# First batch's attention in a fused attention and expert kernel: another order on TensorE, fewer empty products, and the first weight chunk's steps behind the sums

## The chip, the cores and the metric

The kernel runs on one core of one Trainium2 chip, in one launch. The metric is the device time of an execution in microseconds (us). TensorE is called PE in the rows, VectorE DVE, ScalarE ACT, GpSimd POOL, and SyncE, which issues most DMAs, SP.

## The reference, cut to what matters

Three stages follow each other: attention with two kinds of mask over 2 batches, 8 heads, 576 tokens and 64 columns a head; a bilinear layer; and four experts weighted by token.

```python
scores = scale * np.matmul(q, k.transpose(0, 1, 3, 2))
mask_local = (rel >= 0) & (rel < stride)                    # heads 0 to 3, stride 32
mask_strided = (rel >= 0) & (pos[None, :] % stride == pos[:, None] % stride)   # heads 4 to 7
attn = np.exp(scores - max) ; attn = attn / (attn.sum(-1) + 1e-09)
x = np.matmul(attn, v)                                      # 1152 tokens x 512
h = ((x @ w1) * (x @ w2)) @ w3 ;  x = h @ w_out             # 512 -> 1024 -> 1024 -> 512
out += p[:, e:e + 1] * (np.maximum(x @ w1[e], 0.0) @ w2[e]) # four experts
```

The weights of the bilinear layer (w1, w2, w3, w_out) come as 64-bit floats, while attention and experts have 32-bit inputs.

## The kernel before, in words

**Numbers.** Every large product is made of three: an operand is split into a high part (rounded for TensorE, `hi`) and the rest (`lo`), and `mm3` (lines 255 to 259) adds hi times hi, lo times hi and hi times lo into one PSUM bank.

**Weights.** 64-bit weights are worked on as pairs of 32-bit integers, 128 x 1024 at a time (class `Chunk`). The steps of a chunk are `raw_load` (a DMA of 1 MB into one of two `raw` buffers), `round_up` (ACT, L136, on the low words), `magnitude` (ACT, L144, on the high words; for the first chunk DVE, L142), then on DVE `clamp` (L147), `shift` (L150), `sign` (L153) and `add` (L157, which also issues the load of the chunk after next), then `split_hi` on ACT (L164, writes `w_hi`) and `split_lo` on DVE (L174, writes `w_lo`). The generator `work()` (L200) has all of these in one order, and `advance(n)` takes n steps of it wherever the program calls it. So the order on each engine is that of the program text: nothing is scheduled by cost. Chunks are numbered from 0 here; chunks 0 to 7 are w1 and w2 (`c_w12`).

**Attention.** A batch has six pieces (`Chunk4`): three local ones (numbers 0 to 2), then three strided ones (3 to 5). Steps of a piece: `scores` (PE, a mask product and 16 or 24 small ones), `maxima` (DVE, L356 and L361), `exps` (ACT, L367), `sums` (DVE, L374 or L376 to L378), `normalise` (L382; GpSimd in batch 0, DVE in batch 1), `transposes` (PE, L387), `evac` (ACT copies them out of PSUM, L392), `pv` (PE, weights by values, L404 or L413), `put` (ACT, L440, high part of x) and `put_lo` (DVE, L444, low part). `attend(b, s)` (L756) runs the pipeline's step s = 0 to 8: scores of piece s + 1, maxima and exps of s, sums and normalise of s - 1, pv and put of s - 3, transposes and evac of s - 2.

**Order of the work.** Nine steps of batch 0 come first, and in each, TensorE has the scores ahead of pv and transposes, and then some empty products (`keep_warm`, 102 of them in the nine steps after the 14 at the start). Between them `advance` does the first steps of the weights. Then come 32 units (`run_unit`, `ab_block`): unit 2c and 2c + 1 take batch 0 through chunk c, each with 24 products of 128 x 288; each unit takes two steps of the weights, and the steps of batch 1's attention stand after units 2, 4, 5, 7, 8, 10, 11, 13 and 14 (counted from 1). Units 16 to 31 take batch 1 through the chunks. The rest (w3 by w_out, the layer itself, the experts) is not touched.

```python
for k in range(4):
    mm3(acc, c_w12[ft].parts((w * 4 + k) * P, P), (x_hi[:, k, t], x_lo[:, k, t]), k == 0, k == 3)
```

**Limits that tie the engines.** There are 5 PSUM banks for pv, transposes, empty products and units, 3 for scores; each engine does its own instructions in order.

Of the kernel before, what the change touches and what calls it, by code (L numbers as in the profile page):

```python
# [18 lines left out]
P = 128  # L19
# [18 lines left out]
def flat(ap):  # L38
    return ap.rearrange("p a b -> p (a b)")
# [3 lines left out]
def kernel(  # L43
# [13 lines left out]
    nc = tc.nc  # L57
    mm = nc.tensor.matmul
# [13 lines left out]
    def bank(name):  # L72
        return ps.tile([P, 512], F32, tag="ps", name=name)
# [33 lines left out]
    def warm_up():  # L107

        idle = tmp.tile([P, P], F32, tag="pT", name="idle")
        nc.vector.memset(idle, 0.0)  # L110
        nc.scalar.activation(small.tile([P, 1], F32, tag="rec", name="one"), idle[:, :1], AF.Exp)
        zeros = idle.bitcast(BF16)

        def keep_warm(n):
            if n:
                acc = bank("idle")
            for i in range(n):
                mm(acc[:, :2 * P], zeros[:, :P], zeros, start=i == 0, stop=i == n - 1)

        keep_warm(WARM)  # L120
        return keep_warm


    class Chunk:
# [5 lines left out]
        def raw_load(self):  # L130
            self.raw = rawp.tile([P, 1024, 2], I32, tag="raw", name="raw64")
            nc.sync.dma_start(out=flat(self.raw), in_=self.src.bitcast(I32))

        def round_up(self):
            self.low, self.high = self.raw[:, :, 0], self.raw[:, :, 1]
            nc.scalar.activation(self.low, self.low.bitcast(U32), AF.Copy, scale=2.0 ** -29)  # L136

        def magnitude(self):
# [45 lines left out]
    c_w12 = [Chunk(w12[c]) for c in range(8)]  # L184
    c_wout = [Chunk(w_out[c]) for c in range(4)]
    c_w3 = [Chunk(w3T[c]) for c in range(8)]
    live = 8
# [13 lines left out]
    def work():  # L201


        wide = stream[:20]
        wide[0].round_up()
        wide[0].magnitude()
        yield True
        before = None
        for c, after in zip(wide, wide[1:] + [None]):
            if before:  # L210
                while live > 14:
                    yield False
                before.split_hi()
            c.clamp()
            yield True
            if before:
                before.split_lo()
            c.shift()
            yield True
            c.sign()  # L220
            yield True
            if after and c is not wide[0]:
                after.round_up()
                after.magnitude()
            c.add()
            yield True
            before = c
            if c is wide[0]:
                c.split_hi()
                after.round_up()  # L230
                yield True
                c.split_lo()
                yield True
                before = None
                after.magnitude()
        while live > 14:
            yield False
        before.split_hi()
        yield True
        before.split_lo()  # L240
        yield True
        for w in c_e:
            yield from w.work()

    worker = work()

    def advance(n=1):

        return all([next(worker, False) for _ in range(n)])
# [5 lines left out]
    def mm3(acc, lhs, rhs, first, last):  # L255
        (lh, ll), (rh, rl) = lhs, rhs
        mm(acc, lh, rh, start=first, stop=False)  # L257
        mm(acc, lh, rl, start=False, stop=False)  # L258
        mm(acc, ll, rh, start=False, stop=last)  # L259


    x_hi = xp.tile([P, 4, NT], F32R, tag="x_hi", name="x_hi")
    x_lo = xp.tile([P, 4, NT], F32R, tag="x_lo", name="x_lo")
# [185 lines left out]
    def ab_place(b, pair):  # L449
        ab_hi[b, pair] = big[b].tile([P, 2, S], F32R, tag="big", name="ab_hi")  # L450
        ab_lo[b, pair] = big[b].tile([P, 2, S], F32R, tag="big", name="ab_lo")
# [8 lines left out]
    def ab_block(b, ft, n):  # L460
        t = slice(b * S + n * HB, b * S + n * HB + HB)
        pair, late = ft // 2, b == 0 and ft < 6
        ab = tmp.tile([P, HB], F32, tag="pT", name="ab")
        if n == 0 and ft % 2 == 0:
            if late:
                whole[pair] = big[min(pair, 1)].tile([P, 2, S], F32, tag="big", name="ab_f32")
            else:
                ab_place(b, pair)
        if late:
            full = whole[pair][:, ft % 2, n * HB:n * HB + HB]  # L470
        else:
            full = ab
            hi, lo = (x[b, pair][:, ft % 2, n * HB:n * HB + HB] for x in (ab_hi, ab_lo))
        for w in range(2):
            acc = bank("ab_acc")[:, :HB]
            for k in range(4):
                mm3(acc, c_w12[ft].parts((w * 4 + k) * P, P), (x_hi[:, k, t], x_lo[:, k, t]), k == 0, k == 3)
            if w == 0:
                nc.scalar.copy(ab, acc)
            else:  # L480
                nc.vector.tensor_tensor(out=full, in0=acc, in1=ab, op=ALU.mult)
            yield
        if late:
            return
        nc.scalar.copy(hi, ab)
        yield
        nc.vector.tensor_tensor(out=lo, in0=ab, in1=hi.bitcast(F32), op=ALU.subtract)
        yield
# [126 lines left out]
    class Step:  # L615
# [22 lines left out]
        def add(self, out, acc, b):  # L638
            nc.vector.tensor_tensor(out=out, in0=acc, in1=b, op=ALU.add)  # L639

        def first(self, work):

            n = self.half.n
# [6 lines left out]
            self.product(b, "s2", "t2")  # L650
            self.add(u2, b, u1)
            work(1)
            self.product(c, "s3", "t3")
            self.add(u3, c, u2)
# [69 lines left out]
    with tc.manual_schedule():  # L724
        keep_warm = warm_up()
# [20 lines left out]
        chunks = [[Chunk4(3 * g + c, b, g, c) for g in range(2) for c in range(3)] for b in range(B)]  # L746
# [5 lines left out]
        def run_unit():  # L752

            nonlocal done, rest
            b, ft, i = units[done]
            need(c_w12[ft])  # L756
            block = ab_block(b, ft, i)
            for _ in range(2):
                next(rest, None)
                next(block)  # L760
                advance(1)
            rest = block
            done += 1
            if b == i == 1:
                c_w12[ft].free()

        def attend(b, s):

            nonlocal live
            chunk = chunks[b]  # L770
            n = len(chunk)
            if s == 0:
                chunk[0].scores()
            if s + 1 < n:
                chunk[s + 1].scores()
            if s < n:
                chunk[s].maxima()
                chunk[s].exps()
            if 1 <= s <= n:
                chunk[s - 1].sums()  # L780
                chunk[s - 1].normalise()
            if 3 <= s:
                c = chunk[s - 3]
                c.pv()
                c.put()
                c.put_lo()
                if c.g == 0 or b == 0 and c.c > 0:
                    live -= 1
            if 2 <= s < n + 2:
                chunk[s - 2].transposes()  # L790
                chunk[s - 2].evac(nc.scalar.copy)

        for s in range(9):
            attend(0, s)
            advance({4: 2, 5: 3, 6: 1, 7: 1}.get(s, 0))
            keep_warm({4: 20, 5: 14, 6: 12, 8: 16}.get(s, 8))
        advance(4)
        steps = iter(range(9))
        while done < 16:
            run_unit()  # L800
# [13 lines left out]
        for it in range(8):  # L814
# [8 lines left out]
            i = {1: 0, 3: 1, 6: 2}.get(it)  # L823
# [141 lines left out]
```

## Time and profile before

| what | value |
|---|---|
| time, median of 3 runs | 633.12 us (632.18 to 636.05) |
| the profiled execution's own time | 632.63 us |
| its span, first to last instruction | 630.7 us |
| TensorE clock granted, mean | 1.000 |
| busy: PE, DVE, ACT, POOL | 619.2, 450.7, 265.0, 9.9 us |
| moved by DMA | 99.45 MB, mean 158 GB/s |

The span lies inside the time of the execution, with 1.9 us around it. Busy time is a union over the engine's instructions; what an engine waited for is taken from the rows of single instructions.

### The profile page before, as it was taken

How to read it: one execution, taken by the hardware profiler on the slowest of the kernel's cores; microseconds unless marked ns; L12 is line 12 of the kernel's file. 1: busy time of each engine (PE TensorE's matmuls, PEld its weight loads, DVE VectorE, ACT ScalarE, POOL GpSimd, SP SyncE). 2: the span in 40 equal slices, each digit the busy share in tenths (PEclk: the TensorE clock that was granted, in tenths of full speed). 3: DMA queues.
4: the chain of work that ended last, by engine and by line, in shares of the span. 5: the costliest groups of instructions: out<-in, count | busy, mean ns of one | idle time of the engine just before them, and what ended most of it. 6: DMA issues, size and time to landing. Idle time of an engine off the chain costs nothing.

```text
span 630.7 us, 11461 instructions
## 1 busy us (share of the span) xinstructions
PE 619.2 (98%) x4706; PEld 566.1 (90%) x4706; DVE 450.7 (71%) x813; ACT 265.0 (42%) x455; POOL 9.9 (2%) x31
## 2 busy tenths in 40 slices
PE   8899999999999999999999999999999999999997
PEld 6699899999878999999988999898889999999996
DVE  4889996989775224867977887787875666765743
ACT  2555564765654223433344333344433333333320
POOL 4100000000000000000000000000000000000000
PEclk9999999999999999999999999999999999999999
DMA  9973432235442310345344353353497465556411
GB/s 295 268 240 129 135 130 73 77 135 179 147 134 73 128 68 0 134 146 189 133 156 179 134 201 134 136 197 134 143 330 278 150 253 187 212 194 209 137 63 68
DMA packets 28727, 99.45 MB, mean 158 GB/s; under 512 B 2652, under 2 KB 6740, under 8 KB 26116
## 3 DMA queue, kind: packets, MB, share of 16 engines
q1 hardware_dynamic: 28132, 98.14, 44.5%
q8 instruction: 37, 0.61, 0.4%
q10 hardware_dynamic: 544, 0.59, 0.3%
q14 instruction: 14, 0.11, 0.0%
HBM read 79.58 MB, written 19.14 MB: 157 GB/s over the span
## 4 chain that ended last, share of the span: by engine, by line
PE 86%; DVE 4%; ACT 4%; DMA 3%; issue 1%; SPq 1%; DVEq 0%
PE g_acc L257 10%; PE g_acc L258 10%; PE g_acc L259 10%; PE ab_acc L257 5%; PE ab_acc L259 5%; PE ab_acc L258 5%; PE m_a L257 4%; PE m_a L259 4%; PE m_a L258 4%; PE x_acc L257 3%; PE x_acc L258 3%; PE x_acc L259 3%; PE m_b L258 3%; PE m_c L257 3%; PE m_b L257 3%; PE m_c L258 3%
## 5 line engine op out<-in xcount | busy, mean ns | idle before, releaser
L633 ACT ACTIVATE h_hi<-u 128x320 fp32r<-128x320 f32 (+1 forms) x128 | 56.9, 445 | 188.5 <-DVE u L639 188.5
L257 PE MATMUL g_acc<-w_hi,h_hi 128*128 128x512 f32 (+1 forms) x296 | 114.3, 386 | 0.0
L258 PE MATMUL g_acc<-w_lo,h_hi 128*128 128x512 f32 (+1 forms) x296 | 114.2, 386 | 0.0
L259 PE MATMUL g_acc<-w_hi,h_lo 128*128 128x512 f32 (+1 forms) x296 | 113.7, 384 | 0.0
L639 DVE TENSOR_TENSOR u<-m_b,u 128x320 f32<-128x320 f32 (+1 forms) x96 | 40.8, 452 | 52.9 <-PE m_b L259 52.9
L572 DVE TENSOR_TENSOR w_lo<-raw,w_hi 128x768 fp32r<-128x768 f32 x64 | 69.3, 1083 | 12.0 <-ACT w_hi L570 11.9
L257 PE MATMUL ab_acc<-x_hi,w_hi 128*128 128x288 f32 x256 | 76.5, 299 | 1.1 <-ACT pT L392 1.0
L259 PE MATMUL ab_acc<-x_hi,w_lo 128*128 128x288 f32 x256 | 75.4, 294 | 0.0
L258 PE MATMUL ab_acc<-x_lo,w_hi 128*128 128x288 f32 x256 | 75.4, 294 | 0.0
L259 PEld LDWEIGHTS g_acc<-w_hi,h_lo 128*128 128x128 f32 x296 | 55.6, 188 | 11.6
L257 PEld LDWEIGHTS g_acc<-w_hi,h_hi 128*128 128x128 f32 x296 | 55.8, 188 | 8.0
L258 PEld LDWEIGHTS g_acc<-w_lo,h_hi 128*128 128x128 f32 x296 | 55.8, 188 | 7.6
L635 DVE SCALAR_TENSOR_TENSOR h_lo<-u,h_hi 128x320 fp32r<-128x320 f32 (+1 forms) x128 | 57.6, 450 | 3.5 <-ACT h_hi L633 1.7
L570 ACT CAST w_hi<-raw 128x768 fp32r<-128x768 f32 x64 | 59.9, 936 | 0.0
L257 PEld LDWEIGHTS ab_acc<-x_hi,w_hi 128*128 128x128 f32 x256 | 48.0, 188 | 1.8 <-ACT pT L392 1.2
L258 PEld LDWEIGHTS ab_acc<-x_lo,w_hi 128*128 128x128 f32 x256 | 48.1, 188 | 0.0
L259 PEld LDWEIGHTS ab_acc<-x_hi,w_lo 128*128 128x128 f32 x256 | 48.0, 188 | 0.0
L258 PE MATMUL m_b<-b_t,s_hi 128*128 128x320 f32 (+1 forms) x128 | 37.9, 296 | 0.0
L639 DVE TENSOR_TENSOR u<-m_a,u 128x320 f32<-128x320 f32 (+1 forms) x64 | 28.8, 451 | 11.6 <-PE m_a L259 11.6
L572 DVE TENSOR_TENSOR s_lo<-raw,s_hi 128x1024 fp32r<-128x1024 f32 x16 | 19.6, 1225 | 23.2 <-ACT s_hi L570 23.2
L136 ACT ACTIVATE raw<-raw 128x1024 int32<-128x1024 uint32 x20 | 23.4, 1171 | 29.2 <-DMA raw<-in_w3T_dram 19.0
L639 DVE TENSOR_TENSOR u<-m_c,u 128x320 f32<-128x320 f32 (+1 forms) x64 | 28.9, 452 | 4.7 <-PE m_c L259 4.0
(154 smaller groups left out, 1392.7 us busy)
## 6 DMA issues: line engine op xcount, KB each, us to landing
raw<-in_e_dram SPq DMA_DIRECT2D x32, 1024.0 KB
raw<-in_w_dram SPq DMA_DIRECT2D x8, 1024.0 KB
raw<-in_w3T_dram SPq DMA_DIRECT2D x8, 1024.0 KB
stored<-s_hi SPq DMA_DIRECT2D x16, 512.0 KB
stored<-s_lo SPq DMA_DIRECT2D x16, 512.0 KB
s_hi<-stored SPq DMA_DIRECT2D x16, 512.0 KB
s_lo<-stored SPq DMA_DIRECT2D x16, 512.0 KB
raw<-in_w_out_dram SPq DMA_DIRECT2D x4, 1024.0 KB
```

What stands on the lines that cost most here:

```text
L136: nc.scalar.activation(self.low, self.low.bitcast(U32), AF.Copy, scale=2.0 ** -29)
L257: mm(acc, lh, rh, start=first, stop=False)
L258: mm(acc, lh, rl, start=False, stop=False)
L259: mm(acc, ll, rh, start=False, stop=last)
L570: nc.scalar.copy(dst[0], src)
L572: nc.vector.tensor_tensor(out=dst[1], in0=src, in1=dst[0].bitcast(F32), op=ALU.subtract)
L633: nc.scalar.activation(hi, src, AF.Relu)
L635: nc.vector.scalar_tensor_tensor(out=lo, in0=src, scalar=0.0, in1=hi.bitcast(F32), op0=ALU.max, op1=ALU.subtract)
L639: nc.vector.tensor_tensor(out=out, in0=acc, in1=b, op=ALU.add)
```

## The change: what it does

In batch 0 each of the nine steps now has, on TensorE, pv of s - 3, transposes of s - 2, then scores of s + 1, and then the empty products: 6, 8, 12, 12 and 8 in steps 0, 5, 6, 7 and 8 and none in the others (46 in place of 102). `put` and `put_lo` stand behind `sums`, `normalise` and the steps of the weights. The first chunk's steps start in step 5 of the attention in place of step 4 (`magnitude`, `clamp` and `shift` in step 5, `sign` in 6, `add` in 7, `split_hi` and `split_lo` behind step 8), its `round_up` is called in step 6, and 10 steps in place of 11 are done when the units begin. The second chunk's `round_up` moves behind the first one's `split_lo`. The very first of the units' accumulations has its twelve products by kind: four hi by hi, four with x_lo, four with w_lo.

```diff
         def round_up(self):
-            self.low, self.high = self.raw[:, :, 0], self.raw[:, :, 1]
             nc.scalar.activation(self.low, self.low.bitcast(U32), AF.Copy, scale=2.0 ** -29)
...
         wide = stream[:20]
-        wide[0].round_up()
         wide[0].magnitude()
...
             if c is wide[0]:
                 c.split_hi()
-                after.round_up()
                 yield True
                 c.split_lo()
                 yield True
                 before = None
+                after.round_up()
                 after.magnitude()
...
-            for k in range(4):
-                mm3(acc, c_w12[ft].parts((w * 4 + k) * P, P), (x_hi[:, k, t], x_lo[:, k, t]), k == 0, k == 3)
+            parts = [(c_w12[ft].parts((w * 4 + k) * P, P), (x_hi[:, k, t], x_lo[:, k, t])) for k in range(4)]
+            if b == ft == n == w == 0:
+                for i, j in ((0, 0), (0, 1), (1, 0)):
+                    for k, (lhs, rhs) in enumerate(parts):
+                        mm(acc, lhs[i], rhs[j], start=i == j == k == 0, stop=i == 1 and k == 3)
+            else:
+                for k, (lhs, rhs) in enumerate(parts):
+                    mm3(acc, lhs, rhs, k == 0, k == 3)
...
+        first = chunks[0]
+        first[0].scores()
+        first[1].scores()
         for s in range(9):
-            attend(0, s)
-            advance({4: 2, 5: 3, 6: 1, 7: 1}.get(s, 0))
-            keep_warm({4: 20, 5: 14, 6: 12, 8: 16}.get(s, 8))
-        advance(4)
+            if 3 <= s:
+                first[s - 3].pv()
+            if 2 <= s < 8:
+                first[s - 2].transposes()
+            if 2 <= s + 1 < 6:
+                first[s + 1].scores()
+            keep_warm({0: 6, 5: 8, 6: 12, 7: 12, 8: 8}.get(s, 0))
+            if s < 6:
+                first[s].maxima()
+                first[s].exps()
+            if 1 <= s < 7:
+                first[s - 1].sums()
+                first[s - 1].normalise()
+            advance({5: 3, 6: 1, 7: 1}.get(s, 0))
+            if 3 <= s:
+                first[s - 3].put()
+                first[s - 3].put_lo()
+                if s != 6:
+                    live -= 1
+            if 2 <= s < 8:
+                first[s - 2].evac(nc.scalar.copy)
+            if s == 6:
+                c_w12[0].round_up()
+        advance(5)
```

**Place 1: TensorE in steps 2 and 3 of batch 0.** Before, with the scores of pieces 3 and 4 (`sc<-tk,tq 54x54`), the transposes of pieces 0 and 1 (`tp`), values of piece 0 (`o`) and one of each eight empty products:

```order
L343 MATMUL sc<-m_str,i_str 128x432
L350 MATMUL sc<-tk,tq 54x54 x16
L387 MATMUL tp<-ident,p_pair 128x128 x3
L118 MATMUL idle<-idle 128x256
L343 MATMUL sc<-m_str,i_str 128x432
L350 MATMUL sc<-tk,tq 54x54 x16
L404 MATMUL o<-pT,tv_loc 64x32 x24
L387 MATMUL tp<-ident,p_pair 128x128 x3
L118 MATMUL idle<-idle 128x256
```

The same two steps in the changed kernel:

```order
L386 MATMUL tp<-ident,p_pair 128x128 x3
L342 MATMUL sc<-m_str,i_str 128x432
L349 MATMUL sc<-tk,tq 54x54 x16
L403 MATMUL o<-pT,tv_loc 64x32 x24
L386 MATMUL tp<-ident,p_pair 128x128 x3
L342 MATMUL sc<-m_str,i_str 128x432
L349 MATMUL sc<-tk,tq 54x54 x16
```

The scores moved behind the transposes and values of their step, and the empty products of both steps are gone.

**Place 2: ACT around the rounding and magnitude of chunk 6, between units.** Before (`raw_1104` is chunk 6's buffer, `p_pair` the exps of batch 1's piece 4, `x_hi` and `pT` the put of piece 1 and the copy of piece 2's transposes, `ab` a unit's copy, `w_hi` chunk 5's):

```order
L136 ACTIVATE raw_1104<-raw_1104 128x1024
L144 ACTIVATE t<-raw_1104 128x1024
L367 ACTIVATE p_pair<-p_pair 128x8x54
L440 CAST x_hi<-o 128x2x3x32 x2
L392 COPY pT<-tp 128x384
L479 COPY ab<-ab_acc 128x288
L164 CAST w_hi<-t 128x1024
```

In the changed kernel, where chunk 6's buffer is `raw_1059`:

```order
L366 ACTIVATE p_pair<-p_pair 128x8x54
L439 CAST x_hi<-o 128x2x3x32 x2
L391 COPY pT<-tp 128x384
L484 COPY ab<-ab_acc 128x288
L136 ACTIVATE raw_1059<-raw_1059 128x1024
L144 ACTIVATE t<-raw_1059 128x1024
L164 CAST w_hi<-t 128x1024
```

The rounding and the magnitude moved behind the attention's exps, put and copy and behind a unit's copy.

**Place 3: DVE around chunk 6's low part, ahead of unit 12.** Before (`t` of the first row is chunk 7's clamp, `w_lo` is chunk 6's, `rec` and `p_pair` are the sums and normalise of batch 1's piece 5, `x_lo` is piece 3's):

```order
L147 TENSOR_SCALAR t<-t 128x1024
L481 TENSOR_TENSOR ab_f_1305<-ab_acc,ab 128x288
L174 TENSOR_TENSOR w_lo<-t,w_hi 128x1024
L150 TENSOR_SCALAR t<-t 128x1024
L374 TENSOR_REDUCE rec<-p_pair 128x8
L378 RECIPROCAL rec<-rec 128x8
L382 TENSOR_TENSOR p_pair<-p_pair,rec 128x8x54
L444 TENSOR_TENSOR x_lo<-o,x_hi 128x6x18 x4
```

In the changed kernel, with chunk 6's `add` as the first row:

```order
L157 ISA t<-raw_1059,t 128x2048
L486 TENSOR_TENSOR ab_f_1239<-ab_acc,ab 128x288
L147 TENSOR_SCALAR t<-t 128x1024
L373 TENSOR_REDUCE rec<-p_pair 128x8
L377 RECIPROCAL rec<-rec 128x8
L381 TENSOR_TENSOR p_pair<-p_pair,rec 128x8x54
L443 TENSOR_TENSOR x_lo<-o,x_hi 128x6x18 x4
L174 TENSOR_TENSOR w_lo<-t,w_hi 128x1024
L150 TENSOR_SCALAR t<-t 128x1024
```

The low part moved behind seven instructions of the attention; chunk 3's stands in the same way behind the maxima of piece 2 and the sums and normalise of piece 1. From the end of batch 1's attention on, the order is the same as before on every engine.

## Rows read from the trace of the kernel before

**Rows 1.** Stretches: length; PE, PEld, DVE, ACT, POOL busy; clock; DMA share; GB/s.

```profile
0.00:34.00 34.00, 29.85 (x622) 23.79 (x623) 21.91 (x50) 15.28 (x35) 9.68 (x29) 1.00 0.93 284
...
47.00:97.40 50.40, 48.81 (x683) 46.24 (x683) 49.09 (x84) 29.93 (x53) 0.23 (x2) 1.00 0.38 127
100.00:140.00 40.00, 40.00 (x304) 40.00 (x303) 32.15 (x50) 24.59 (x39) 0.00 (x0) 1.00 0.28 97
```

**Rows 2.** Timeline, TensorE, batch 0: start, us, instruction, [idle before, releaser].

```profile
16.80 0.91 PE L350 MATMUL sc<-tk,tq 64*18 64x18 f32 x32
...
18.17 0.90 PE L404 MATMUL o<-pT,tv_loc 64*64 64x32 f32 x47 [0.43 <-issue]
...
25.02 1.25 PE L118 MATMUL idle<-idle 128*128 128x256 bf16 x10 [1.44 <-issue]
...
31.52 0.90 PE L413 MATMUL o<-pT,tv_str 54*64 54x54 f32 x32 [0.66 <-ACT pT L392]
...
32.35 1.92 PE L118 MATMUL idle<-idle 128*128 128x256 bf16 x16
...
34.03 0.38 PE L257 MATMUL ab_acc<-x_hi,w_hi 128*128 128x288 f32 x1
```

**Rows 3.** Timeline, other engines, batch 0.

```profile
9.98 0.83 POOL L382 TENSOR_TENSOR p_pair<-p_pair,rec 128x384 f32<-128x384 f32 x1 [4.71 <-DVE rec L378]
...
16.97 0.61 DVE L361 TENSOR_TENSOR p_pair<-sc,mx 128x432 f32<-128x432 f32 x1
...
21.94 0.61 DVE L361 TENSOR_TENSOR p_pair<-sc,mx 128x432 f32<-128x432 f32 x1
22.46 0.60 DVE L374 TENSOR_REDUCE rec<-p_pair 128x8 f32<-128x440 f32 x1
...
24.94 1.22 DVE L153 SCALAR_TENSOR_TENSOR t<-raw,t 128x1024 int32<-128x1024 int32 x1
...
28.10 1.10 DVE L444 TENSOR_TENSOR x_lo<-o,x_hi 128x108 fp32r<-128x108 f32 x4
28.17 1.05 ACT L164 CAST w_hi<-t 128x1024 fp32r<-128x1024 f32 x1
...
29.12 1.15 ACT L136 ACTIVATE raw<-raw 128x1024 int32<-128x1024 uint32 x1
...
30.83 0.63 ACT L392 COPY pT<-tp 128x512 f32<-128x512 f32 x1
...
32.46 0.67 ACT L440 CAST x_hi<-o 128x108 fp32r<-128x108 f32 x4 [0.99 <-PE o L413]
```

**Rows 4.** Timeline, DVE, beside the units.

```profile
44.36 0.56 DVE L361 TENSOR_TENSOR p_pair<-sc,mx 128x384 f32<-128x384 f32 x1
45.53 0.69 DVE L147 TENSOR_SCALAR t<-t 128x1024 f32<-128x1024 f32 x1 [0.61 <-ACT t L144]
...
47.18 1.23 DVE L174 TENSOR_TENSOR w_lo<-t,w_hi 128x1024 fp32r<-128x1024 f32 x1 [0.49 <-ACT w_hi L164]
...
83.53 1.21 DVE L174 TENSOR_TENSOR w_lo<-t,w_hi 128x1024 fp32r<-128x1024 f32 x1
...
86.66 1.20 DVE L444 TENSOR_TENSOR x_lo<-o,x_hi 128x108 fp32r<-128x108 f32 x4
```

**Rows 5.** Timeline, ACT, beside the units.

```profile
43.33 1.16 ACT L136 ACTIVATE raw<-raw 128x1024 int32<-128x1024 uint32 x1 [3.80 <-DMA raw<-in_w_dram]
44.38 1.12 ACT L144 ACTIVATE t<-raw 128x1024 f32<-128x1024 f32 x1
45.41 0.51 ACT L367 ACTIVATE p_pair<-p_pair 128x384 f32<-128x384 f32 x1
45.82 0.38 ACT L479 COPY ab<-ab_acc 128x288 f32<-128x288 f32 x1
```

**Rows 6.** Timeline, TensorE: values and transposes ahead of unit 11.

```profile
82.28 0.82 PE L413 MATMUL o<-pT,tv_str 54*64 54x54 f32 x32 [0.61 <-ACT pT L392]
83.04 0.66 PE L387 MATMUL tp<-ident,p_pair 128*128 128x128 f32 x4
```

More of the change, by code (lines that the diff above doesn't have):

```diff
@@ L132, in raw_load @@
             nc.sync.dma_start(out=flat(self.raw), in_=self.src.bitcast(I32))
+            self.low, self.high = self.raw[:, :, 0], self.raw[:, :, 1]
         def round_up(self):
-            self.low, self.high = self.raw[:, :, 0], self.raw[:, :, 1]
             nc.scalar.activation(self.low, self.low.bitcast(U32), AF.Copy, scale=2.0 ** -29)
```

## The prediction

> **What bounds the kernel now.** I read the stretches first, then the waits, then single rows in order of time. The page's 98% for TensorE hides three regimes. In the first 34 us (batch 0's attention) no engine is full: TensorE shows 29.85 us, of which 102 empty products are part, DVE 21.91 [rows 1]. It is a loop through all engines: scores, maxima, exps, sums, normalise on GpSimd, transposes, copy, values, put. From 47 to 97.4 us DVE is busy for 49.09 of 50.40 us while TensorE has only 1.6 us idle: both are nearly full, and the weights' steps and batch 1's attention share DVE [rows 1]. From 100 to 140 us TensorE is full and DVE has 7.85 us idle: TensorE sets the pace there [rows 1]. So the change works in the first regime, and what it gains must be carried through the second, where DVE has nothing to give away.
>
> **The head, part by part.** 56 empty products go, at 0.125 us each (1.25 us for ten [rows 2]) 7 us of TensorE; most of it lay beside the loop. Where they stood on the path: ten at 25.02 and sixteen at 32.35, ahead of the first unit at 34.03 [rows 2]. I walk the new order with the rows' durations. Nothing moves until GpSimd has normalised piece 0, at 10.8 [rows 3]. Transposes (0.55) go first now, then the scores of piece 3 (0.91 and about 0.4 for the mask [rows 2]): they end at 12.75, and DVE subtracts piece 3 by 14.05, which is some 0.8 later than before. This is the price of the new order. Sums 1.0, low parts of piece 0 0.6 and maxima 0.6 bring the subtraction of piece 4 to 16.25, before 16.97 [rows 3]; the next cycle (subtraction, 0.5 of exps [rows 5], put 0.54, low part, maxima) brings piece 5 to 19.15, before 21.94 [rows 3]. DVE then has sums (0.6 [rows 3] and 0.25 for the reciprocal), magnitude, clamp and shift (0.7 each, as the clamp of [rows 4]), low part of piece 2 (0.6), sums (0.8): 24.0; sign 1.22 [rows 3], low part of piece 3 1.1 [rows 3], add 1.22: 27.4. That is when it ended before too (24.94 and twice 1.22 [rows 3]), so the load of chunk 2 that it issues, and the loads of batch 1's values behind that on SP, start when they did. Beside it: normalise 24.15 to 25.0, transposes 0.66 [rows 6], copy 0.63 [rows 3] behind piece 4's put to 26.6; the twelve empty products ahead of the last values wait for a PSUM bank (low part of piece 3) and end at 27.2; values 0.9 to 28.1, put 0.67 to 28.75, and now `w_hi` stands behind that put on ACT: 1.05 to 29.8 [rows 3]. First product at 29.85 in place of 34.03: 4.2 us early. `w_lo` comes at 31.07, behind the first eight products by kind, which end at 30.9; without the new order of these twelve TensorE would stand from the third one on, some 0.9 us. So unit 0 ends at 33.25, 4.0 early.
>
> An unknown: the unbroken runs of TensorE at 17.7 and 23.6 have gaps of 0.43 and 1.44 us with no releaser [rows 2]. The new run has the like places at 17.2 (scores of piece 5) and 24 (empty products). Bounds: nothing, or both, 1.87 us; I take 0.4, since the second falls beside DVE's work.
>
> [...]
>
> **What the units give back.** At the start of the units 10 steps of the weights are done in place of 11, and the second chunk's rounding and magnitude on ACT stand behind `w_hi` at 29.8. They end at 31.95 (1.05 and 1.12 [rows 5]); clamp, shift, sign, add 3.85 to 35.8; unit 0's product 0.4, clamp 0.6; chunk 1's `w_hi` at 36.9, `w_lo` 36.95 to 38.1; shift, product, sign 2.15, maxima 1.2, add 1.2: 42.55. Before, the same instructions were done at 44.92 [rows 4]. So DVE is 2.4 us ahead there, TensorE 4.0.
>
> Then the waits. Before, DVE had two after this point, 0.61 and 0.49 us, and none from 47 to 84 [rows 4]. In the new order the rounding and magnitude of a chunk stand behind that step's exps, put, transposes' copy and a unit's copy on ACT, where they stood ahead of them. Chunk 3: exps end 0.55 after the subtraction (41.4), copy 0.4, rounding 1.05, magnitude 1.12 [rows 5]: 44.4, while DVE is free at 42.9: a wait of 1.5, and chunk 2's `w_hi` is later by 0.35 for it. The load behind it lands earlier: issued at 35.9, 5.2 us after which it was there before [rows 5]. Later chunks: exps 0.56, put 0.5, copy 0.45, copy 0.4, rounding and magnitude 2.2 make 4.1 us from subtraction to clamp on ACT; on DVE sums 0.85, normalise 0.5, low part 0.55, add 1.2, product 0.4 make 3.5. So each such clamp waits 0.3 to 0.6: chunks 4 to 7 cost 0.1, 0.3, 0.4, 0.55, and chunk 5's `w_hi` 0.4. Sum 3.6, before 1.1: DVE's 2.4 shrink to -0.1.
>
> Last the order itself. Chunk 6's `w_lo` was written by 84.7 [rows 4], 2.4 us ahead of the third product of unit 12, which reads it first: TensorE had it at 87.1 (values at 82.28, transposes to 83.7 [rows 6], unit 11 of 24 times 0.132, two more). Now sums, normalise and four low parts (2.5 us) stand ahead of `w_lo`. The equal set of work was done at 87.16 before (87.8 less one shift of 0.61) [rows 4], so now at 87.2. TensorE, up to 2.2 us ahead by unit 10, stands 1.9 us there and starts the rest of unit 12 at 87.2 in place of 87.1. A smaller stand of 2 us is due at unit 6 (chunk 3's `w_lo`, behind 2.65 us of attention, at 57.2 in place of 55.3). After that the order is the old one, TensorE is full again, and no wait remains that a lead could fill.
>
> **The sum.** On the profiled execution's own 632.63 us: head -4.0, given back +4.1, gaps +0.4: 633.1. That run is 0.5 below the median of the three shown, so against the median this reads as no change. One per cent, 6.3 us, is about what a measurement of this kernel can tell from no change.
>
> **The rivals.** *The lead is kept.* If ACT keeps up, the clamps' waits (2.85 us) and the `w_hi` ones (0.75) go, and DVE keeps 3.5 us at unit 12: 629.1. For it speaks that ACT is busy for only 29.93 of 50.4 us [rows 1]; against it that each part of ACT's queue between subtraction and clamp has a releaser that is on DVE or TensorE itself. A half of it gives 630.9. Chance 0.27.
>
> *ACT's queue decides (slower).* The place is `round_up` of chunks 4 to 7. It waits on the put ahead of it, and that on TensorE's values. From the point where TensorE stands for `w_lo` (units 6 and 12), values, put and copies come later, so rounding, clamp and the next `w_lo` do too; each clamp then waits about 1.1 in place of 0.3 to 0.55 us. Four chunks: 2.5 us: 635.6. For it: `w_lo` was only 2.4 us early [rows 4, 6]. Against it: copies of a unit cost 0.38 [rows 5] and ACT has 20 us free. Chance 0.15.
>
> *The clock falls (slower).* [...] The new run leaves TensorE idle for about 1.45 us before 10.9 and 0.9 before 29.85 and has no empty products from 8.3 to 20. [...] Chance 0.05. [...]
>
> *The change does nothing in the head.* If loads, not the loop, set it (DMA share 0.93 [rows 1]), the first product stays near 33 and the units then lose: 635. Chance 0.03; the releasers in the rows of the head are engines or nothing, not DMAs [rows 2, 3].
>
> **How the numbers follow.** The forecast (632 to 634.3) has 0.50, the three above 0.27, 0.15, 0.05, the last 0.03. The range 630.0 to 635.3 leaves out half of the first rival, and the far part of the slower ones. Faster by over 1% (under 626.3) would need more than the whole lead of the head: 0.03. Slower by over 1% (over 638.9) only with the clock and ACT together: 0.03. Within 1%: 0.94.
>
> **What would show it.** In the new profile: first unit product near 30, granted clock 1.00 in 0 to 34; subtraction of pieces 4 and 5 near 16.3 and 19.2; a DVE wait of about 1.5 us on ACT's magnitude near 43; waits of TensorE on `w_lo` of about 2 us near 55 and 85; from there on TensorE's times equal to those of before within 1 us. I am wrong if TensorE has no such waits and unit 16 starts 2 us or more early (rival one), or if the first product stands later than 32.

## The result, and the profile after

| | before | changed |
|---|---|---|
| median, first set of five each | 633.19 us (632.18 to 636.05) | 639.99 us (638.98 to 640.82) |
| profiled execution, span | 632.63, 630.7 us | 638.98, 636.8 us |
| mean granted clock of that execution | 1.000 | 0.995 |

The ratio is 1.0105 with a 95% interval of 1.0081 to 1.0129: about 1% slower. A later set of ten on another occasion gave 636.75 us, 1.0059 (1.0038 to 1.0080). The forecast of 633.1, and its range to 635.3, were too low for both.

The stretches answer to [rows 1]; three of 4 us in the head are added (columns as there):

```profile
0.00:34.00 34.00, 25.27 (x567) 19.81 (x567) 20.71 (x49) 12.95 (x32) 10.76 (x29) 0.90 0.81 243
16.00:20.00 4.00, 1.19 (x35) 0.79 (x28) 2.24 (x6) 1.37 (x4) 0.96 (x2) 0.88 1.00 206
20.00:24.00 4.00, 2.94 (x74) 2.84 (x74) 1.63 (x3) 0.32 (x1) 0.00 (x0) 0.50 1.01 345
24.00:28.00 4.00, 4.00 (x54) 3.17 (x53) 3.89 (x8) 2.43 (x9) 1.18 (x1) 0.77 0.71 216
47.00:97.40 50.40, 45.26 (x626) 42.25 (x626) 45.15 (x80) 28.74 (x50) 0.23 (x2) 1.00 0.38 128
100.00:140.00 40.00, 40.00 (x306) 40.00 (x303) 31.50 (x54) 24.91 (x41) 0.00 (x0) 1.00 0.31 107
```

Two things are new. From 16 to 20 us TensorE is busy for 1.19 us only, and from 20 to 24 its granted clock is 0.50. And from 47 to 97.4 us, where DVE had 1.3 us idle, it now has 5.25, and TensorE 5.1 in place of 1.6.

TensorE's timeline in the head, which answers to [rows 2]:

```profile
13.37 0.66 PE L403 MATMUL o<-pT,tv_loc 64*64 64x32 f32 x30 [0.81 <-issue]
...
16.90 0.29 PE L349 MATMUL sc<-tk,tq 64*18 64x18 f32 x9
21.05 1.13 PE L349 MATMUL sc<-tk,tq 64*18 64x18 f32 x20 [3.86 <-issue]
...
22.03 1.51 PE L403 MATMUL o<-pT,tv_loc 64*64 64x32 f32 x46
...
24.37 1.76 PE L118 MATMUL idle<-idle 128*128 128x256 bf16 x8
...
34.46 0.79 PE L479 MATMUL ab_acc<-x_hi,w_hi 128*128 128x288 f32 x4 [0.64 <-ACT w_hi L164]
```

In the middle of the scores of piece 5 TensorE stands for 3.86 us with no releaser. Values behind it take 1.51 us in place of 0.86, eight empty products 1.76 in place of 1.04. The first unit product comes at 34.46, where 29.85 was forecast. DVE and GpSimd in the head, as [rows 3]:

```profile
16.39 0.61 DVE L360 TENSOR_TENSOR p_pair<-sc,mx 128x432 f32<-128x432 f32 x1
...
22.33 0.61 DVE L355 TENSOR_REDUCE mx<-sc 128x8 f32<-128x432 f32 x1 [3.87 <-PE sc L349]
22.98 0.61 DVE L360 TENSOR_TENSOR p_pair<-sc,mx 128x432 f32<-128x432 f32 x1
...
28.15 1.17 DVE L153 SCALAR_TENSOR_TENSOR t<-raw,t 128x1024 int32<-128x1024 int32 x1
...
28.37 1.72 POOL L381 TENSOR_TENSOR p_pair<-p_pair,rec 128x432 f32<-128x432 f32 x1 [2.71 <-DVE rec L377]
```

Up to the gap the walk held: piece 4 is subtracted at 16.39 (forecast 16.25), piece 5 at 22.98 (forecast 19.15) because its scores came 3.87 us late. Beside the units, DVE as in [rows 4] (the last row, the sum of the expert probabilities `den`, marks the end of that regime; it stood at 102.96 before), and TensorE (the last row is the first product of unit 16):

```profile
48.98 0.70 DVE L147 TENSOR_SCALAR t<-t 128x1024 f32<-128x1024 f32 x1 [1.43 <-ACT t L144]
49.92 1.23 DVE L174 TENSOR_TENSOR w_lo<-t,w_hi 128x1024 fp32r<-128x1024 f32 x1 [0.25 <-ACT w_hi L164]
...
65.97 0.69 DVE L147 TENSOR_SCALAR t<-t 128x1024 f32<-128x1024 f32 x1 [0.46 <-ACT t L144]
...
78.06 0.69 DVE L147 TENSOR_SCALAR t<-t 128x1024 f32<-128x1024 f32 x1 [0.41 <-ACT t L144]
...
87.44 0.69 DVE L147 TENSOR_SCALAR t<-t 128x1024 f32<-128x1024 f32 x1 [0.52 <-ACT t L144]
...
90.47 1.24 DVE L174 TENSOR_TENSOR w_lo<-t,w_hi 128x1024 fp32r<-128x1024 f32 x1
...
109.05 0.19 DVE L721 TENSOR_REDUCE den<-pn 128x9 f32<-128x36 f32 x1 [1.87 <-DMA pn<-in_probs_dram]
```

```profile
61.77 0.40 PE L258 MATMUL ab_acc<-x_hi,w_lo 128*128 128x288 f32 x1 [1.84 <-DVE w_lo L174]
...
91.75 0.40 PE L258 MATMUL ab_acc<-x_hi,w_lo 128*128 128x288 f32 x1 [1.54 <-DVE w_lo L174]
...
106.45 0.29 PE L256 MATMUL ab_acc<-x_hi,w_hi 128*128 128x288 f32 x1
```

Before, the third product of unit 12, which reads chunk 6's `w_lo` first, and unit 16's first product stood at:

```profile
87.00 0.29 PE L259 MATMUL ab_acc<-x_hi,w_lo 128*128 128x288 f32 x1
...
101.59 0.29 PE L257 MATMUL ab_acc<-x_hi,w_hi 128*128 128x288 f32 x1
```

The waits from 34 to 140 us (engine, line, releaser: sum, times, longest) show the same two pairs:

```profile
DVE t L147 <- ACT t L144: 4.1, 6, 1.4
...
PE ab_acc L258 <- DVE w_lo L174: 3.4, 2, 1.8
```

So the units hold the waits that the forecast named, of nearly the size that it gave them (1.5 for chunk 3's clamp, about 2 and 1.9 for `w_lo`), and the head holds one that it did not.

### The profile page after: what moved, and what is told of

Its sections match the earlier page's. It is cut to its first block, busy times and chain, and to the rows that moved or that the text cites. A ratio compares the mean times of both kernels' runs of the same rounds, so it can differ in the third digit from the quotient of the medians.

```text
span 636.8 us, 11354 instructions
## 1 busy us (share of the span) xinstructions
PE 615.5 (97%) x4650; PEld 562.1 (88%) x4650; DVE 451.2 (71%) x813; ACT 264.5 (42%) x455; POOL 11.0 (2%) x31
## 4 chain that ended last, share of the span: by engine, by line
PE 73%; DVE 11%; ACT 7%; DMA 5%; issue 4%; POOL 0%; DVEq 0%; SPq 0%; ACTq 0%; POOLq 0%
PE g_acc L256 10%; PE g_acc L257 10%; PE g_acc L258 10%; PE m_a L256 4%; PE m_a L258 4%; PE m_a L257 4%; DMA raw<-in_w3T_dram 3%; PE x_acc L256 3%; PE x_acc L257 3%; PE x_acc L258 3%; PE m_b L257 3%; PE m_c L256 3%; PE m_b L256 3%; PE m_c L257 3%; PE m_c L258 3%
## 5 line engine op out<-in xcount | busy, mean ns | idle before, releaser
L258 PE MATMUL ab_acc<-x_hi,w_lo 128*128 128x288 f32 x252 | 74.5, 296 | 3.4 <-DVE w_lo L174 3.4
```

## The experiments: the weights' steps

Theory A says that there are two costs, TensorE's missing instructions in the head and the moved steps beside the units; B that the low clock behind the removed empty products is the loss; C that the new order on TensorE is. First each half alone. The changed kernel with the steps of before:

```diff
+        wide[0].round_up()
         wide[0].magnitude()
...
-            advance({5: 3, 6: 1, 7: 1}.get(s, 0))
+            advance({4: 2, 5: 3, 6: 1, 7: 1}.get(s, 0))
...
-        advance(5)
+        advance(4)
```

> The changed kernel with the weights' steps as they were before (first chunk's steps from step 4 of the attention on, 11 steps done when the units begin, rounding and magnitude where they stood). Theory A (TensorE runs out of instructions for 3.9 us in the head, which eats the gain there; the moved weight steps cost some 5 us beside the units, which is a separate cost): the gap of about 3.9 us and the clock of 0.50 stay, first unit product near 34, TensorE's waits on w_lo near 60 and 85 us go, time 633 to 636. Theory B (the low clock behind the removed empty products is the whole loss): no gain from the steps, 639 to 641. Theory C (the new order of TensorE, scores behind values and transposes, is the loss): 639 to 641 too, with the waits on w_lo replaced by others.

Measured 634.53 us, 1.0026 (1.0003 to 1.0048): most of the loss is gone. What is left has an interval that just leaves out 1; its cause stays open. The gap was 1.12 us, the clock 0.57 from 20 to 24, and the waits on `w_lo` were gone. The reverse, the kernel before with the change's steps alone (the same edits turned round):

> The kernel before with only the weights' steps of the change (first chunk's steps from step 5 on, 10 steps done when the units begin, rounding and magnitude behind put, copies and the split); TensorE's order and all 102 empty products as before. Theory A: first unit product within 1 us of 34.0, then waits on w_lo of some 2 us twice, 636.5 to 639, which is 4 to 6 us over the kernel before. Theories B and C: within 1.5 us of the kernel before.

639.10 us, 1.0089 (1.0059 to 1.0118). First unit product at 33.38, 0.65 us earlier than before, and yet the sum of the probabilities at 108.05, 5.1 us later. The steps alone make a loss of this size, with all empty products and the old order in place; B and C are not needed for it. Which step? One number in the changed kernel:

```diff
-        advance(5)
+        advance(6)
         steps = iter(range(9))
```

> The changed kernel with one number changed: 11 steps of the weights done when the units begin, as before, in place of 10 (chunk 1's add and the load that it issues, with chunk 2's rounding and magnitude, come ahead of unit 0 again). Theory A, sharpened (the steps' cost is this one step: every later step stands one place further back against batch 1's attention): den's load lands DVE at 103 to 105 in place of 109, no waits on w_lo near 60 and 88, 633 to 636. Theory D (the cost is that chunk 1's rounding and magnitude stand behind the split on ACT): 638 to 640 as the changed kernel.

> The kernel with 11 steps of the runs before once more, to see how much its head differs between executions. The profile before had the packet at 15.2 us, a gap of 0.85 us and the first product at 30.70. If the packet's time is by chance: the same or 17.5, 2.8 and 33.5 to 34.5. Median 632 to 634.5, as before.

633.12 us, 0.9987 (0.9967 to 1.0006), and again 633.97, 1.0002 (0.9985 to 1.0018). The same number in the kernel before, `advance(3)` for `advance(4)` ahead of the units:

> The kernel before with one number changed: 10 steps done when the units begin in place of 11, nothing else. Theory A, sharpened: 4 to 5.5 us slower than the kernel before on the same chip, with TensorE's waits on w_lo of chunks 3 and 6. Theory D: within 1.5 us of the kernel before.

637.75 us beside 633.00, 1.0059 (1.0030 to 1.0088), with waits on `w_lo` of 2.7 us in sum. One step less costs 3.7 us by the ratio (4.75 between the medians) in the old order too; D, that chunk 1's rounding and magnitude behind the split are the cost, falls. Twelve steps, `advance(7)`:

> The changed kernel with 12 steps done when the units begin. 10 steps cost 3 to 5 us over 11 because each later step stood behind a stretch of batch 1's attention. If the place against the attention is what counts, 12 need not gain on 11: chunk 2's clamp then stands ahead of unit 0's product on DVE, 632.5 to 635. If simply more steps done early were worth 4 us a step: 628 to 630.

634.81 us, 1.0032 (1.0012 to 1.0051): no gain on 11. Its profiled head also had a gap of 3.59 us, so this median alone does not tell the place of the steps from the head; that steps are worth 4 us each is excluded.

TensorE's own times tell the two apart, whatever the head was. From the first unit product to unit 16's took 70.4 to 74.5 us in the seven profiles with ten steps (72.0 in the changed kernel), 67.6 to 69.5 in the nine with eleven (67.6 before) and 71.5 with twelve. What follows unit 16 took 529.1 to 530.4 us in fourteen of these seventeen profiles; in the other three it took 531.3 to 532.3.

The twelve products by kind, undone with 11 steps (`mm3` for all four parts):

> The kernel with 11 steps, but with the first accumulation's twelve products in the old order (three for each of four parts) in place of by kind. My prediction counted 0.9 us for it at unit 0: TensorE stands from the third product on until w_lo is written. All theories: unit 0 later by 0.6 to 0.9 us, and the time the same within 0.7 us of the run with 11 steps, because DVE and the loads of chunk 3 set what follows.

633.23 us, 0.9999 (0.9980 to 1.0018). TensorE's timeline there:

```profile
31.82 0.40 PE L256 MATMUL ab_acc<-x_hi,w_hi 128*128 128x288 f32 x1 [0.63 <-ACT w_hi L164]
...
33.09 0.40 PE L258 MATMUL ab_acc<-x_hi,w_lo 128*128 128x288 f32 x1 [0.73 <-DVE w_lo L174]
```

It stands 0.73 us for `w_lo`, as counted, and the time does not show it.

## The experiments: the gap in the head

What I take TensorE to wait for in such a gap is a packet on an instruction queue in the DMA view (queue, kind: packets, MB, share of 16 engines). From 17 to 18 us in the changed kernel, and from 13 to 14 in a kernel told below, where the scores of piece 5 have no gap:

```profile
q8 instruction: 1, 0.02, 9.2%
```

```profile
q8 instruction: 1, 0.02, 7.7%
```

The packet of the changed kernel begins at 17.9 and takes 1.5 us (9.2% of 16), and TensorE goes on at 21.05. All times of packets below are those at which they begin.

The gaps stand at a fixed distance in instructions: each of these 32-bit products stands twice in PE's rows and twice in those of its weight loads (24 products are x48), and counted so the gaps at 12.56 and 17.2 us lie 254 apart (127 rows of each kind), and those of [rows 2] 252; such a stretch is called a block below. To move them, the changed kernel with the empty products of before:

```diff
-            keep_warm({0: 6, 5: 8, 6: 12, 7: 12, 8: 8}.get(s, 0))
+            keep_warm({4: 20, 5: 14, 6: 12, 8: 16}.get(s, 8))
```

> The changed kernel with the empty products of before (8, 8, 8, 8, 20, 14, 12, 8, 16 in steps 0 to 8; 102 in place of 46). Theory A (TensorE's instructions come in blocks whose arrival sets the gaps; the steps' cost is separate): 26 more empty products of two instructions stand ahead of the scores of piece 5, so the second gap moves 52 instructions forward in the program, from the scores of piece 5 to the end of the values of piece 1 or its transposes, and is 1 to 3 us long; the clock stays 1.00; the steps' cost stays, 638 to 640. Theory B (the low clock behind the removed empty products is the main loss): 634 to 636.

638.42 us, 1.0074 (1.0051 to 1.0097), clock 1.00, first product 33.75. The second gap stood in the values of piece 1, 13 records before their end, about where 52 instructions forward lead; but it was 0.22 us long, less than expected: the packet began at 15.6, and TensorE came to the place 0.8 us later than in the changed kernel. 56 empty products more do not take the loss away: B falls again.

Then the loads. The first try held chunk 1 and batch 1 back, behind a small GpSimd write into chunk 1's buffer in step 4:

```diff
         load_v_str(0)
-        load_next()
-        load_qk(1, 0)
-        load_v_loc(1, 0)
...
                 first[s - 1].normalise()
+            if s == 4:
+                load_next()
+                load_qk(1, 0)
+                load_v_loc(1, 0)
...
+            if self is c_w12[1]:
+                nc.gpsimd.memset(self.raw[:, :1, :].bitcast(F32), 0.0)
             nc.sync.dma_start(out=flat(self.raw), in_=self.src.bitcast(I32))
```

> The changed kernel with the load of weight chunk 1 and the loads of batch 1 behind it held until GpSimd has normalised piece 3 (about 18.8 us; issued from 14.5 us on so far), so that fewer data stand in the DMA engines' way between 14 and 19 us. Theory A: the instruction packet of the 17th us comes at 15 to 16, the gap of 3.86 us in the scores of piece 5 shrinks to under 2 us, the clock stays 1.00, the first unit product comes near 31, and with the steps' cost still there the time is 634 to 637. If the gap doesn't hang on the other loads: gap 3.5 us or more, first product near 34.5, 639 to 641. Theory B expects the low clock to come all the same, since the empty products are still missing: first product near 33, 638 or more.

> The changed kernel with both: the weights' steps as before and the loads held as in the run before. Theory A: both losses go and the head's gain is left, first product near 31, 628 to 632, the first version under the kernel before. Theories B and C: 636 or more.

> The changed kernel with 11 steps and with the loads of chunk 1 and batch 1 held to step 4. Theory A, sharpened: where the gap is near 1 us (packet of the 15th us), chunk 1's add and so the load of chunk 3 is 2 us earlier than before, 630 to 632; where it is 3 us (packet of the 17th us), 633 to 635; the median between, 631 to 634.5. Theories B and D: 637 or more.

Measured 637.13 us, 1.0067 (1.0042 to 1.0092); with the old steps 634.42, 1.0027 (1.0012 to 1.0042); with 11 steps 633.76, 0.9998 (0.9977 to 1.0019). The second expectation was missed clearly, the first just. The packet began at 15.5, 17.3 and 17.3 us and the gaps were 1.12, 3.04 and 2.77: this hold did not touch what delays the packet. Nor is a gap of one length a mark of one kernel:

> The changed kernel itself once more. If the packet's time is by chance, the profile may show the packet near 15.5, a gap of about 1 us and the first product near 31 to 31.5 this time, and a time of 636 to 638 in that execution (the ten steps' 4 to 5 us stay); else the packet near 17.9 and 639 to 641 again. Median 637 to 640.

Median 636.75, just under what was expected. The profile of the changed kernel this time (634.86 us):

```profile
18.48 0.76 PE L349 MATMUL sc<-tk,tq 64*18 64x18 f32 x21 [1.40 <-issue]
...
31.46 0.79 PE L479 MATMUL ab_acc<-x_hi,w_hi 128*128 128x288 f32 x4 [0.63 <-ACT w_hi L164]
```

And the kernel before with 10 steps, its 102 empty products in place, shows a long gap where [rows 2] has 0.43:

```profile
20.65 1.50 PE L404 MATMUL o<-pT,tv_loc 64*64 64x32 f32 x47 [2.88 <-issue]
```

Its clock was 0.55 from 20 to 24. In the fourteen profiled executions where data fill the DMA engines (a share of 0.97 to 1.10 from 12 to 16 us), the packet begins between 15.2 and 17.9 us, and in all of them TensorE starts the next block 1.4 to 1.7 us after the packet's end. What decides where in that span it begins, no run shows. To empty the engines at 13 us, the changed kernel with 11 steps and all loads behind piece 2's values held to step 3 (15.4 us):

> The changed kernel with 11 steps, and every load behind the values of piece 2 (chunk 0, the strided values, chunk 1, batch 1) held until GpSimd has normalised piece 2 (about 15.4 us), so that the DMA engines run dry near 14.6 us. Theory A (the second gap in TensorE's instructions is the time in which the instruction packet waits among data in the DMA engines): the packet, asked for near 13.2 us, lands by 15.0 in every execution, the gap in the scores of piece 5 is under 0.7 us, clock 1.00, first product 30 to 31.5 (the strided values or chunk 0 may now come late by up to 1 us), 630.5 to 633. If the packet's delay has another cause: packet at 17.5 in some executions, gap to 3 us and a clock of 0.5 behind it, 632 to 635.

634.96 us, 1.0028 (1.0012 to 1.0044), over what was expected. The packet began at 14.2 and the scores of piece 5 had no gap, but the strided values came too late:

```profile
22.09 0.32 PE L414 MATMUL o<-pT,tv_str 54*64 54x54 f32 x4 [1.32 <-DMA tv_str<-in_v_str_dram]
24.23 0.67 PE L414 MATMUL o<-pT,tv_str 54*64 54x54 f32 x28 [1.82 <-DMA tv_str<-in_v_str_dram]
```

So these were left ahead, and only the weights and batch 1 held (the hold is on chunk 0's buffer):

```diff
-        load_next()
         load_v_str(0)
-        load_next()
-        load_qk(1, 0)
-        load_v_loc(1, 0)
...
+            if s == 3:
+                load_next()
+                load_next()
+                load_qk(1, 0)
+                load_v_loc(1, 0)
```

> The changed kernel with 11 steps; the strided values are loaded ahead of the weights, and chunk 0, chunk 1 and batch 1 are held until GpSimd has normalised piece 2 (about 15.4 us), so that neither the instruction packet nor the strided values come late. Theory A: packet by 15.0, no gap of over 0.7 us in the scores of piece 5, clock 1.00, no waits on the strided values, first product 29.8 to 30.7, time 630.5 to 632.5, 0.1 to 0.4% under the kernel before. If the head's gain is worth nothing whatever the gap: 633 to 634.

> The changed kernel as it is (10 steps) with the loads in the order and with the hold of e14. This takes the gap and the low clock out of the head and leaves the ten steps. My prediction's walk then should hold for the head (first product 29.9 to 30.7), and its sum without the term for the gaps was 632.7. Theory A, that the walk mis-sized what the units give back by about 1 us and left out the clock's falls at TensorE's waits for w_lo: 634 to 636.5. If the gap in the head had been the whole error of the prediction: 632 to 633.5.

With 11 steps 632.03 us, 0.9987 (0.9969 to 1.0005); with the change's 10 steps 634.87, 1.0043 (1.0027 to 1.0059). The packets began at 13.9 and 14.2. TensorE's timeline with 11 steps, scores of piece 5 and first unit product:

```profile
16.63 0.91 PE L351 MATMUL sc<-tk,tq 64*18 64x18 f32 x32
...
30.41 0.79 PE L481 MATMUL ab_acc<-x_hi,w_hi 128*128 128x288 f32 x4 [0.63 <-ACT w_hi L166]
```

No gap, clock 1.00 in the whole head. With 10 steps the first product came at 30.67, and later TensorE's timeline and stretches show what the steps do alone:

```profile
57.97 0.40 PE L260 MATMUL ab_acc<-x_hi,w_lo 128*128 128x288 f32 x1 [1.84 <-DVE w_lo L176]
...
88.88 0.40 PE L260 MATMUL ab_acc<-x_hi,w_lo 128*128 128x288 f32 x1 [1.51 <-DVE w_lo L176]
```

```profile
60.00:70.00 10.00, 10.00 (x203) 9.35 (x203) 8.32 (x16) 5.25 (x9) 0.11 (x1) 0.88 0.32 107
...
90.00:100.00 10.00, 10.00 (x119) 9.53 (x118) 8.22 (x14) 6.41 (x14) 0.00 (x0) 0.85 0.31 107
```

After each of the two stands the clock falls for a while in this execution (0.88 from 60 to 70 us, 0.85 from 90 to 100). It need not: in the changed kernel's profile it was 1.00 in the same stretches, behind stands of 1.84 and 1.54 us. From the first unit product to unit 16's the three profiles with ten steps, the change's order of steps and no fall there took 72.0 us, one with a single fall 73.5, two with both 74.4 and 74.5, so 1.2 to 1.5 us a fall. The start of `w_lo` by chunk, in us, lays the two costs side by side:

| chunk | before | changed | no gap, 10 steps | no gap, 11 steps |
|---|---|---|---|---|
| 0 | 31.58 | 34.44 | 30.65 | 30.39 |
| 2 | 47.18 | 49.92 | 46.13 | 45.24 |
| 3 | 55.27 | 60.50 | 56.70 | 53.32 |
| 6 | 83.53 | 90.47 | 87.60 | 81.58 |
| sum of the probabilities | 102.96 | 109.05 | 106.83 | 100.87 |

From nearly one head the two right columns are 0.9 us apart at chunk 2, 3.4 at chunk 3, and end 6.0 apart.

## Why the prediction was wrong, point by point

**The gaps: the step that failed.** "Bounds: nothing, or both, 1.87 us; I take 0.4, since the second falls beside DVE's work." The two gaps made 4.67 us, and the second fell into scores that DVE waited for. I took the gaps' lengths in one execution as a property of the place. I read them as what is left of a transfer: a packet of kind instruction (0.02 MB) stands in the DMA view beside the data's, TensorE started its next block 1.4 to 1.7 us after that packet's end where data fill the engines, and with fewer data in the way (a share of 0.22 to 0.73 in place of 0.97 to 1.10) the packet came at 13.9 to 14.2 us in place of 15.2 to 17.9 and the gap went. By this reading a TensorE that is faster up to the end of its block waits longer for the next. How long also changes between executions: the second profile of the same kernel had gaps of 0.54 and 1.40 us, 1.94 in all, beside my bound of 1.87. So a part of the 4.67, and of the distance between the two sets (639.99 and 636.75), is chance.

**The head, -4.0, was +0.43 in the profiled execution** (34.46 for 34.03); a first product later than 32 was my own sign of being wrong. The walk itself was right but for one term: without the gap the first product came at 30.41 and 30.67 for 29.85. What is left, 0.6 and 0.8 us, fits GpSimd's normalise of piece 5, which I took at 0.85 us, near its old length (0.92), and which took 1.72 us beside DVE's sign; TensorE's transposes wait 0.8 us for it, in these two runs as well.

**"The clock falls", chance 0.05**, happened in the head of the profiled execution: 0.50 from 20 to 24 us and 0.77 from 24 to 28. Missing empty products alone did not bring it down: with 46 and a gap of 0.85 us, or none with the weights held, it stayed at 1.00. With all loads held, and no gap in the scores of piece 5, it was 0.61 from 24 to 28 us, behind the waits of 1.32 and 1.82 us for the strided values. Behind gaps of 2.77 us and more it fell in all five profiles that have them, one with all 102 (0.55). Between these it is open whether empty products matter: behind 1.1 to 1.4 us it fell soon after in three of five profiles with 46 (0.57, 0.57 and 0.66 from 20 to 24 us), while behind 1.44 and 1.71 us, ending near 25 us, it stayed at 1.00 in two profiles with 102.

**What the units give back, +4.1, was 4.4 up to unit 16** (106.45 for 101.59, less 0.43) and 5.9 to the end (638.98 less 632.63 less 0.43). Places and waits were right: of the waits that I counted, the clamps of chunks 3 to 7 took 2.8 us and the two on `w_hi` 0.5, for 2.85 and 0.75. From the first unit product to the rest of unit 12 I counted 57.35 us (29.85 to 87.2), and it took 57.29 (34.46 to 91.75; before, 52.97). "After that the order is the old one ... and no wait remains" held to 0.1 us up to unit 16. The other 1.5 us came later, 1.3 of them where TensorE stood for ACT, at 153.42 (0.71 us) and 191.81 (0.64); no run shows that these belong to the change, and the time behind unit 16 differs by as much between the other profiles. What I did not count is that the clock falls behind the two stands in some executions. In the kernel without the gap four executions with a clock of 1.000 took 634.04 to 634.57 us, four at 0.995 took 636.49 to 636.84.

**The sum.** The head was off by 4.0 (+0.43 for -4.0 and +0.4), the units by 0.3 and what follows them by 1.5: 633.1 and 5.8 make the 638.9 of the profiled execution. Had the gap been away, the forecast without its 0.4 for gaps, 632.7, would still have met 634.87: 0.8 us of that are the normalise, and each fall of the clock behind a stand adds 1.2 to 1.5.

**The rivals.** ACT's queue deciding (635.6) did not come: the clamps of chunks 4 to 7 waited 0, 0.46, 0.41 and 0.52 us, not 1.1 each, and unit 12 was no later behind the head than forecast. The change doing nothing in the head (first product near 33, 635) is nearer to the 34.46 of the profiled execution, and loads do come into it; but what stood behind them, as I read it, was the packet, and with the loads held the loop itself gave 30.41 and 30.67. The lead kept (629.1) did not come even with a clean head and 11 steps: 632.03 cannot be told from before. In its profile 3.6 us at the first product were 1.95 at unit 16 (99.64 for 101.59). There ACT's rounding of chunk 3 waits 3.59 us for its load, as it waited 3.80 in [rows 5]; that this is the next limit is read from the waits and not tested.

## What to carry to other kernels

A gap with no releaser that stands at equal counts of instructions I read here as what is left of a supply, not as a cost of its place: ask what the faster order will do to it, and what else the DMA engines carry ahead of it; holding loads that nobody needs yet took it away here. In a pipeline whose steps are taken in turn with another stream, one step more or less ahead of the loop moves every later step behind a different neighbour; here that single number was worth 3 to 5 us. The edit of the head gained nothing that could be measured: with 11 steps in its own order the time was that of before, and with the old steps (634.53, and 634.42 with loads held) 0.26% longer, with intervals that just leave out 1.

## What the runs showed of the hardware

Counted from where TensorE begins the block before (12.8 to 13.7 us), the packet began about 1.1 us later in the three profiles where the DMA engines' share from 12 to 16 us was 0.22 to 0.73, and 1.9 to 4.6 us later in the fourteen where it was 0.97 to 1.10. In these fourteen TensorE started the next block 1.4 to 1.7 us after the packet's end.

In the changed kernel GpSimd's normalise of a strided piece took 0.91 us beside attention work on DVE:

```profile
17.90 0.91 POOL L381 TENSOR_TENSOR p_pair<-p_pair,rec 128x432 f32<-128x432 f32 x1 [2.44 <-ACT x_hi L439]
```

It took 1.72 when DVE's sign had begun 0.22 us before it (28.15 and 28.37): the sign ended at 29.32, and the normalise 0.77 us after that. In the two kernels with the weights held it took 1.72 as well, the sign had begun 0.23 and 0.22 us before it, and the normalise ended 0.78 and 0.77 us after the sign.
